# A transformer block on one core: first tiles normalized apart, the last outputs taken straight from PSUM, and the planner's costs adjusted

## The chip, the cores and the metric

The kernel runs on one core of one Trainium2 chip. The metric is the device time of one launch in microseconds (us). Lower is better. TensorE multiplies matrices into PSUM (PE in the profile; its weight loads are PEld), ScalarE (ACT) computes exponentials and tanh, VectorE (DVE) does elementwise work, GpSimd (POOL) one small power operation, SyncE (SP) issues transfers. The first measurement of the kernel before was 1119.43 us, the median of three runs (1118.68 to 1120.59).

## The reference

One block on x of 2048 tokens by 1024 channels, in bf16: layer norm, attention with 32 heads of 32 channels, output projection, residual; then layer norm, a feed-forward net of width 3584 with tanh-gelu, residual.

```python
x = A_x
h = x + _A_ref(_layernorm(x, axis=-1), A_wqkv, A_wo)
h2 = h + _B_ref(_layernorm(h, axis=-1), B_w1, B_b1, B_w2, B_b2)
return h2
# _A_ref: qkv = x @ wqkv; softmax(q k^T * 32**-0.5) v; @ wo
# _B_ref: gelu(x @ w1 + b1) @ w2 + b2
```

## The kernel before

The kernel is a graph of tasks, each with an engine, its instructions, and a **planned duration**. When the kernel is built, a list scheduler (the planner) walks through the graph with these durations and fixes the order of the instructions on each engine. The planner never measures: if an instruction takes longer or shorter than planned, the order stays and some engine waits.

```python
MM = 0.2195                       # a 512-column matmul; 0.0015 is added below

def c_act(n, ap_bias=False):      # ScalarE
    return 0.100 + (0.093 if ap_bias else 0.0) + n / 1200.0
...
def mm(g, lhsT, rhs, start, stop, reads, cols=(0, 512)):
    c0, c1 = cols
    occ = MM * (c1 - c0) / 512.0 + 0.0015
```

The planner gives TensorE a ready score matmul (`qk`) first, then a ready product with V (`pv`), then background work: projections, ffn1, ffn2. A score matmul becomes ready, in the plan, when the exponentials before it have freed their place in PSUM (the memory that TensorE writes to). So how much background work is let in between two score matmuls follows from how long the planner believes the exponentials take.

```python
if qk is not None:
    return qk
if pv is not None and not (...):
    ...
    return pv
if bg is not None:
    ...
    return bg
```

One attention round is one batch of 8 score matmuls, two exponentials of 128x1024 on ScalarE, a VectorE add of the halves of the result, 8 matmuls with V and 4 with ones (the softmax sums):

```python
pe(fns, 0.224, reads=[B_KT[g][r], B_QT[self.slot]], ..., kind="qk", mode="row")
for q in range(2):
    act(lambda a, u=u, q=q: a.activation(PT[:, s, 2*q:2*q+2, :], psum[:, 2*u:2*u+2, :], ACT.Exp, ...), 1024, ...)
```

The other places that the change touches, with cuts:

```python
for i in range(8):                # head: two tiles of x per step
    tts = [2 * i, 2 * i + 1]
    ln_tiles(tts, 0)
...
def ffn2(R, c, j, t, tail=False):
    grp = group(f"f2.{c}.{j}{t}")
    ...
    mm(grp, two_row[:, :], b2t[:, 512*j:512*j+512], True, False, ...)      # the bias as a matmul
    for fc in range(FC): mm(grp, gT[...], w[...], False, fc == FC - 1, ...)
    dve(... scalar_tensor_tensor(o, psum[:, grp.bank, :], 0.5, hch[...], ALU.mult, ALU.add) ...)
```

The softmax here doesn't subtract the row's maximum and nothing guards it: scores larger than these inputs give would overflow.

Of the kernel before, what the change touches and what calls it, by code (L numbers as in the profile page):

```python
# [7 lines left out]
ACT = mybir.ActivationFunctionType  # L8
# [304 lines left out]
def build_kernel(nc, A_x, A_wqkv, A_wo, B_w1, B_b1, B_w2, B_b2, out):  # L313
# [81 lines left out]
    pt_hi = top.cur  # L395
    NOT = 2
# [60 lines left out]
    MM = 0.2195  # L457
# [7 lines left out]
    def c_act(n, ap_bias=False):  # L465
        return 0.100 + (0.093 if ap_bias else 0.0) + n / 1200.0
# [38 lines left out]
    def dve(fn, occ, reads=(), writes=(), prio=0):  # L505
        return gr.add(E.DVE, fn, occ, 0.08, reads, writes, prio)
# [28 lines left out]
    cnt = {"ln": 0}  # L535

    def layer_norm(tiles, prio):
# [5 lines left out]
        for k, (x_ap, B_x, o_ap, B_o) in enumerate(tiles):  # L543
            for c in range(2):
                dve(lambda v, c=c, k=k, x_ap=x_ap: v.bn_stats(st_l[:, i + k, 6 * c:6 * c + 6], x_ap[:, 512 * c:512 * c + 512]),
                    0.68, reads=[B_x[c % len(B_x)]], writes=[B_stl[i + k]], prio=prio)
            dve(lambda v, k=k: v.bn_aggr(mv_l[:, i + k, :], st_l[:, i + k, :]), 0.2,
                reads=[B_stl[i + k]], writes=[B_mv[i + k]], prio=prio)
# [8 lines left out]
        for k, (x_ap, B_x, o_ap, B_o) in enumerate(tiles):  # L557
            dve(lambda e, k=k, x_ap=x_ap, o_ap=o_ap: e.tensor_scalar(
                o_ap, x_ap, mvr[:, i + k, :], rden[:, i + k, :], ALU.subtract, ALU.mult), 0.58,
                reads=B_x + [B_mvr[i + k], B_rden[i + k]], writes=[B_o], prio=prio)  # L560

    def transposes(g, src_ap, B_src, dst_ap, B_dst, evac):
        for dc in range(DC):
            grp_pe(g, lambda p, dc=dc: p.transpose(psb[:, g.bank, dc * P:(dc + 1) * P], src_ap[:, dc * P:(dc + 1) * P], ident[:]),  # L564
                   0.064, [B_src, B_ident], "full")
        if evac == "act":
            act(lambda a: a.activation(dst_ap, psb[:, g.bank, :].rearrange("p (dc t) -> p dc t", dc=DC), ACT.Copy), 1024,
                reads=[g.buf], writes=[B_dst], prio=-1)
        else:
            dve(lambda v: v.tensor_copy(dst_ap, psb[:, g.bank, :].rearrange("p (dc t) -> p dc t", dc=DC)), c_dve_ps(1024),  # L570
                reads=[g.buf], writes=[B_dst])
# [21 lines left out]
    def ln_tiles(tts, prio):  # L593
        layer_norm([x_slot(tt) + (xb[:, tt % NXB, :], B_xb[tt % NXB]) for tt in tts], prio)
# [55 lines left out]
    class Job:  # L650

        def __init__(self, g, c, bank=None, direct=False):
# [3 lines left out]
            self.needs = [t for b in B_V[g] for t in b.w] + B_OT[c % NOT][g].r + B_OT[c % NOT][g].w  # L656
            self.r = 0
            self.dens = []

        def round(self):  # L660
# [16 lines left out]
            pe(fns, 0.224, reads=[B_KT[g][r], B_QT[self.slot]], writes=[B_ps[2 * u + k] for u in us for k in range(2)],  # L677
# [5 lines left out]
            if not self.direct:  # L683
# [11 lines left out]
            t = pe(fns, 0.224, reads=B_PT[s] + [B_V[g][r]], writes=[self.buf], kind="pv", mode="col")  # L695
            pvs.append(t)
            job_of[t] = self
            self.dens.append((r, s if self.direct else z))
# [6 lines left out]
        def den(self, r, s):  # L705
            fns = []
            srcs = [PT[:, s, :, 0:256], PT[:, s, :, 256:512]] if self.direct else [PS[:, s, :, :]]
# [5 lines left out]
            pe(fns, 0.112 * len(srcs), reads=(B_PT[s] if self.direct else [B_PS[s]]) + [B_ones], writes=[self.buf], kind="pv", mode="col")  # L713

        def finish(self):
# [5 lines left out]
            dve(lambda v: v.tensor_copy(OS[:, f, :], psum[:, self.bank, 0:256]), c_dve_ps(256),  # L721
                reads=[self.buf], writes=[B_OS[f]], prio=-1)
# [4 lines left out]
            dve(lambda v: v.tensor_tensor(OT[:, c % NOT, g, :], OS[:, f, :], RT[:, f, :], ALU.mult), c_dve(256),  # L727
                reads=[B_OS[f], B_RT[f]], writes=[B_OT[c % NOT][g]])

# [90 lines left out]
    def ffn2(R, c, j, t, tail=False):  # L820
# [3 lines left out]
        grp = group(f"f2.{c}.{j}{t}")  # L824
        grp.soft = {d for _, _, d in ws}
        grp.dmas = [d for _, _, d in ws]
        grp.soft |= soft[c]
        grp.gate = [gate[c]]
        mm(grp, two_row[:, :], b2t[:, 512 * j:512 * j + 512], True, False, [B_two, B_b2t])
        for fc in range(FC):  # L830
            w, bw, _ = ws[fc // 4]
            mm(grp, gT[:, c % 2, fc, t * P:t * P + P], w[:, fc % 4, :], False, fc == FC - 1, [B_gT[c % 2][fc], bw])
        o, bo = R.os.next()
        dve(lambda v, j=j, t=t, o=o, grp=grp: v.scalar_tensor_tensor(
            o, psum[:, grp.bank, :], 0.5, hch[:, c % 2, t, 512 * j:512 * j + 512], ALU.mult, ALU.add),
            c_dve_ps(512), reads=[grp.buf, B_hch[c % 2][2 * t + j]], writes=[bo], prio=-2)
        dma(rows(out2, c, t, j), o, P * 1024, reads=[bo], prio=0)
# [31 lines left out]
    for i in range(8):  # L869
        tts = [2 * i, 2 * i + 1]  # L870
        ln_tiles(tts, 0)
# [92 lines left out]
    R2.os = Ring(ring(tail, "b_os", 2, 512, BF))  # L964
# [9 lines left out]
    for t in range(2):  # L974
        for j in range(2):
            wo_group(R2, L, j, t, ws[j])
        ln2_tile(R2, L, t, "act")
    for jt in F2:
        ffn2(R1, L - 1, *jt)
# [168 lines left out]
```

## Time and profile before

| | us |
|---|---|
| span of the profiled run (granted clock 1.000) | 1115.2 |
| first exponential starts | 16.9 |
| last exponential starts | 1044.0 |
| attention, first to last exponential | 1027.1 |
| tail, last exponential to the end | 71.2 |

I split the span at the first and the last exponential throughout, because these two marks exist in every version, whatever its order. The columns of a stage line are: the stretch, its length, then busy time and count for PE, PEld, DVE, ACT and POOL, the granted TensorE clock, the DMA share and GB/s. The kernel before, attention and tail:

```profile
16.90:1044.00 1027.10, 989.17 (x19567) 539.85 (x19568) 777.11 (x1388) 1009.90 (x1090) 13.52 (x20) 1.00 0.51 148
1044.00:1115.20 71.20, 67.77 (x469) 41.40 (x461) 35.02 (x53) 21.31 (x39) 1.09 (x2) 1.00 0.44 132
```

Subtract busy from length: in attention PE is idle 37.9 us and ACT 17.2, in the tail PE 3.4.

### The profile page before, as it was taken

The page shows a single profiled execution, that of the slowest core. Times are in us where ns is not written, and L with a number is a line of the kernel's source. Part 1 is how long each engine was busy: PE and PEld are TensorE (multiplying, and loading weights), DVE is VectorE, ACT ScalarE, POOL GpSimd, SP SyncE. Part 2 cuts the span into 40 slices and gives each one's busy share as a digit, 9 for nine tenths or more (in the row PEclk, how much of TensorE's full clock was granted, in tenths as well). Part 3 has the DMA queues.
Part 4 walks back from the last instruction along what each step waited for, and adds up shares of the span by engine and source line. Part 5 has one row for each costly group of instructions (what it writes and reads, how often), then busy time and mean ns, then how long its engine had stood idle before and what let it go on. Part 6 is the DMA issues. An engine that isn't in the chain of part 4 may idle for free.

```text
span 1115.2 us, 43935 instructions
## 1 busy us (share of the span) xinstructions
PE 1071.1 (96%) x20150; PEld 592.7 (53%) x20150; DVE 823.3 (74%) x1470; ACT 1035.3 (93%) x1131; POOL 18.0 (2%) x36
## 2 busy tenths in 40 slices
PE   8999999999999899999999999999999999999998
PEld 6646464644444555554565455455545554564483
DVE  7465756667767897788798788878887887797662
ACT  4889999999999999999999999999999999999550
POOL 1000000000000000000000000000000000000000
PEclk9999999999999999999999999999999999999999
DMA  6960100013234536375558464674747377688770
GB/s 190 200 162 4 40 4 3 4 48 106 66 101 139 166 110 209 100 242 146 176 157 247 131 200 145 189 230 121 241 117 226 113 230 209 202 229 239 229 241 20
DMA packets 248101, 165.38 MB, mean 148 GB/s; under 512 B 35947, under 2 KB 245867, under 8 KB 247916
## 3 DMA queue, kind: packets, MB, share of 16 engines
q1 hardware_dynamic: 247916, 162.57, 49.7%
q8 instruction: 158, 2.59, 1.0%
q14 instruction: 27, 0.22, 0.1%
HBM read 152.05 MB, written 7.34 MB: 143 GB/s over the span
## 4 chain that ended last, share of the span: by engine, by line
PE 73%; ACT 17%; DVE 7%; issue 1%; DMA 1%; POOL 0%; DVEq 0%; POOLq 0%
PE ps L495 28%; PE ps L498 21%; ACT PT L681 16%; PE ps L673 11%; PE ps L691 8%; PE ps L710 4%; DVE PS L686 3%; DVE gT L795 1%; PE ps L863 1%; ACT a_th L813 1%; DMA q_scratch<-stg 1%; PE ps L564 1%; DVE gT L814 0%; DVE a_sq L811 0%; DVE DT L719 0%
## 5 line engine op out<-in xcount | busy, mean ns | idle before, releaser
L681 ACT ACTIVATE PT<-ps 128x1024 bf16<-128x1024 f32 x1024 | 962.0, 1039 | 15.1 <-PE ps L673 8.8
L686 DVE TENSOR_TENSOR PS<-PT 128x1024 bf16<-128x1024 bf16 x496 | 328.4, 684 | 76.4 <-PE ps L710 40.1
L498 PE MATMUL ps<-hnT,w1r 128*128 128x256 bf16 x1632 | 208.0, 274 | 9.0 <-DVE gT L795 6.8
L673 PE MATMUL ps<-QT,KT 32*128 32x256 bf16 x4096 | 203.5, 273 | 10.9 <-ACT PT L681 9.6
L495 PE MATMUL ps<-w2r,gT 128*32 128x512 bf16 x2992 | 204.0, 381 | 0.2 <-DVE gT L814 0.2
L691 PE MATMUL ps<-PT,V 128*32 128x256 bf16 x4096 | 185.4, 274 | 4.6 <-ACT PT L681 2.7
L498 PEld LDWEIGHTS ps<-hnT,w1r 128*128 128x128 bf16 x1632 | 146.5, 98 | 63.2 <-issue 35.6
L673 PEld LDWEIGHTS ps<-QT,KT 32*128 32x128 bf16 x4096 | 61.0, 92 | 160.8 <-ACT PT L681 100.4
L710 PE MATMUL ps<-PS,ones 128*32 128x256 bf16 x1984 | 139.2, 276 | 0.9 <-DVE PS L686 0.5
L495 PE MATMUL ps<-xnT,Wall 128*32 128x512 bf16 x1888 | 128.9, 381 | 4.2 <-DVE KT L577 1.5
L691 PEld LDWEIGHTS ps<-PT,V 128*32 128x32 bf16 x4096 | 97.1, 96 | 55.0 <-issue 17.7
L495 PEld LDWEIGHTS ps<-w2r,gT 128*32 128x32 bf16 x2992 | 69.9, 96 | 64.2 <-issue 23.0
L795 DVE TENSOR_TENSOR gT<-ps,b1f 128x512 bf16<-128x512 f32 x98 | 67.2, 686 | 26.1 <-PE ps L498 25.3
L710 PEld LDWEIGHTS ps<-PS,ones 128*32 128x32 bf16 x1984 | 51.7, 95 | 42.6 <-DVE PS L686 23.8
L495 PEld LDWEIGHTS ps<-xnT,Wall 128*32 128x32 bf16 x1888 | 45.0, 96 | 47.5 <-issue 14.0
L814 DVE SCALAR_TENSOR_TENSOR gT<-a_th,gT 128x1024 bf16<-128x1024 f32 x49 | 59.7, 1219 | 13.5 <-ACT a_th L813 13.5
L495 PE MATMUL ps<-w1r,OT 128*32 128x512 bf16 x896 | 59.7, 381 | 2.7 <-DVE hch L755 1.1
L811 DVE SCALAR_TENSOR_TENSOR a_sq<-a_sq,gT 128x1024 bf16<-128x1024 bf16 x49 | 59.8, 1220 | 0.7
L495 PE MATMUL ps<-Wall,xnT 128*32 128x256 bf16 x1536 | 51.4, 273 | 1.3 <-DVE KT L577 0.8
L813 ACT ACTIVATE a_th<-a_sq 128x1024 f32<-128x1024 bf16 x49 | 51.9, 1060 | 0.4 <-DVE a_sq L811 0.2
L719 DVE STREAM_TRANSPOSE DT<-ps 128x256 f32<-128x256 f32 x64 | 28.6, 447 | 24.2 <-PE ps L710 24.2
L495 PEld LDWEIGHTS ps<-Wall,xnT 128*32 128x32 bf16 x1536 | 38.3, 97 | 9.2 <-issue 7.2
(81 smaller groups left out, 625.0 us busy)
## 6 DMA issues: line engine op xcount, KB each, us to landing
w2r<-in_B_w_dram SPq DMA_DIRECT2D x105, 512.0 KB, 6.1
w1r<-in_B_w_dram SPq DMA_DIRECT2D x102, 512.0 KB, 4.5
w1r<-in_A_wo_dram SPq DMA_DIRECT2D x28, 512.0 KB, 4.6
wk<-in_B_w_dram SPq DMA_DIRECT2D x9, 512.0 KB, 5.5
xrb<-in_A_x_dram SPq DMA_DIRECT2D x16, 256.0 KB, 4.2
Wall<-in_A_wqkv_dram SPq DMA_DIRECT2D x16, 256.0 KB, 5.2
wv<-in_B_w_dram SPq DMA_DIRECT2D x8, 512.0 KB, 7.3
a_x<-in_A_x_dram SPq DMA_DIRECT2D x28, 128.0 KB, 3.7
```

The lines of the kernel that those rows point to most:

```text
L495: fns.append(lambda p, j=j: p.matmul(dst(32 * j, 32 * j + 32), lhsT[:, 32 * j:32 * j + 32], rhs, start=start, stop=stop, tile_position=(0, ...
L498: t.alt = [lambda p: p.matmul(dst(0, P), lhsT, rhs, start=start, stop=stop, skip_group_check=True)]
L673: fns.append(lambda p, i=i, hh=hh, r0=r0: p.matmul(psum[:, 2 * us[hh // 2] + hh % 2, 256 * i:256 * i + 256], KT[r0:r0 + 32, g, 256 * r + P ...
L681: act(lambda a, u=u, q=q: a.activation(PT[:, s, 2 * q:2 * q + 2, :], psum[:, 2 * u:2 * u + 2, :], ACT.Exp, bias=0.0, scale=SCALE), 1024, r ...
L686: dve(lambda v: v.tensor_tensor(PS[:, z, :, :], PT[:, s, :, 0:256], PT[:, s, :, 256:512], ALU.add), c_dve(1024, 2), reads=B_PT[s], writes= ...
L691: fns.append(lambda p, i=i, hh=hh: p.matmul(psum[32 * hh:32 * hh + 32, self.bank, 0:256], V[:, g, 2 * r + i, 32 * hh:32 * hh + 32], PT[:, ...
L710: fns.append(lambda p, i=i, hh=hh, src=src: p.matmul(psum[32 * hh:32 * hh + 32, self.bank, 256:512], ones32[:, :], src[:, hh, :], start=False,
L719: dve(lambda v: v.transpose(DT[:, f, :], psum[:, self.bank, 256:512]), c_dve_ps(256), reads=[self.buf], writes=[B_DT[f]], prio=-1)
L795: gate[c] = dve(lambda v, xh=xh, fc=fc, grp=grp: v.tensor_tensor(xh, psum[:, grp.bank, :].rearrange("p (f n) -> p f n", f=2), b1f[:, fc:fc ...
L811: dve(lambda v: v.scalar_tensor_tensor(v4(sq), v4(sq), C2, xh, ALU.add, ALU.mult), c_dve(n), reads=[b_sq] + b_xh, writes=[b_sq], prio=1)
L813: act(lambda a: a.activation(th, sq, ACT.Tanh, bias=0.0, scale=K2 / 2), n, reads=[b_sq], writes=[b_th], prio=-1, kind="tanh")
L814: t = dve(lambda v: v.scalar_tensor_tensor(xh, v4(th), 1.0, xh, ALU.add, ALU.mult), c_dve(n), reads=[b_th] + b_xh, writes=b_xh, prio=1)
```

## The change

Its stated intent: bring the first projection forward (normalize the first tile alone, let idle ScalarE compute the sums of the second), shorten the path behind the last exponential, take the bias matmuls out of the TensorE-bound tail, and end on a smaller eviction. The diff also moves the planner's durations closer to measured ones, which its headline does not say. Cut to its core:

```diff
-    MM = 0.2195
+    MM = 0.2140
-        return 0.100 + (0.093 if ap_bias else 0.0) + n / 1200.0      # c_act
+        return 0.090 + (0.093 if ap_bias else 0.0) + n / 1200.0
-            pe(fns, 0.224, ...kind="qk") ; pe(fns, 0.224, ...kind="pv") ; pe(fns, 0.112 * len(srcs), ...)
+            pe(fns, 0.217, ...)          ; pe(fns, 0.217, ...)          ; pe(fns, 0.1085 * len(srcs), ...)
...
+            if k in on_act:                                  # sums of one tile on ScalarE
+                for f, fn in enumerate((ACT.Copy, ACT.Square)):
+                    act(... a.activation(junk, x_ap, fn, scale=1.0, accum_out=st_l[:, i + k, f:f + 1]) ...)
+                (three small VectorE steps: mean, -mean^2, variance)
-        ln_tiles(tts, 0)
+        if i == 0:
+            ln_tiles(tts[:1], LEAD_PRIO)
+            first = ln_tiles(tts[1:], LEAD_PRIO, (0,))
+        else:
+            ln_tiles(tts, 0, (), first)
...
+            direct = self.direct or (self.final and r == 7)  # last head: no add of halves on VectorE
+            (last head: output multiplied from PSUM, no copy OS)
...
+        n = 256 if tail and (j, t) == F2[-1] else 512        # last group in two halves
+            if not tail:
                 mm(grp, two_row[:, :], b2t[:, 512 * j:512 * j + 512], True, False, ...)
+            h_ap, b_h = (hb[:, t, at], B_hb[t]) if tail else (hch[...], ...)   # hb = hch + b2, made on VectorE
```

More of the change, by code (lines that the diff above doesn't have):

```diff
@@ L395, in build_kernel @@
     pt_hi = top.cur
+    junk = PT[:, NPT - 1, 0:2, :]
+    B_junk = B_PT[NPT - 1][0]
     NOT = 2
@@ L503, in act, with dve @@
         return gr.add(E.Activation, fn, c_act(n, ap_bias), 0.14, reads, writes, prio, kind)
-    def dve(fn, occ, reads=(), writes=(), prio=0):
-        return gr.add(E.DVE, fn, occ, 0.08, reads, writes, prio)
+    def dve(fn, occ, reads=(), writes=(), prio=0, after=()):
+        return gr.add(E.DVE, fn, occ, 0.08, reads, writes, prio, after=after)
     def pool(fn, occ, reads=(), writes=(), prio=0):
@@ L535, in build_kernel, with layer_norm @@
     cnt = {"ln": 0}
-    def layer_norm(tiles, prio):
+    LEAD_PRIO = -4
+    def layer_norm(tiles, prio, on_act=(), after=()):
         n = len(tiles)
@@ L543, in layer_norm @@
         for k, (x_ap, B_x, o_ap, B_o) in enumerate(tiles):
+            if k in on_act:
+                for f, fn in enumerate((ACT.Copy, ACT.Square)):
+                    act(lambda a, k=k, x_ap=x_ap, f=f, fn=fn: a.activation(
+                        junk, x_ap, fn, scale=1.0, accum_out=st_l[:, i + k, f:f + 1]), 1024 + 112,
+                        reads=B_x, writes=[B_stl[i + k], B_junk], prio=-1)
+                dve(lambda v, k=k: v.tensor_scalar(mv_l[:, i + k, 0:1], st_l[:, i + k, 0:1], 1.0 / D, None, ALU.mult), 0.12,
+                    reads=[B_stl[i + k]], writes=[B_mv[i + k]], prio=prio)
+                dve(lambda v, k=k: v.scalar_tensor_tensor(st_l[:, i + k, 2:3], mv_l[:, i + k, 0:1], -1.0, mv_l[:, i + k, 0:1], ALU.mult, ALU.mult),
+                    0.12, reads=[B_mv[i + k]], writes=[B_stl[i + k]], prio=prio)
+                dve(lambda v, k=k: v.scalar_tensor_tensor(mv_l[:, i + k, 1:2], st_l[:, i + k, 1:2], 1.0 / D, st_l[:, i + k, 2:3], ALU.mult, ALU.add),
+                    0.12, reads=[B_stl[i + k]], writes=[B_mv[i + k]], prio=prio)
+                continue
             for c in range(2):
                 dve(lambda v, c=c, k=k, x_ap=x_ap: v.bn_stats(st_l[:, i + k, 6 * c:6 * c + 6], x_ap[:, 512 * c:512 * c + 512]),
-                    0.68, reads=[B_x[c % len(B_x)]], writes=[B_stl[i + k]], prio=prio)
+                    0.68, reads=[B_x[c % len(B_x)]], writes=[B_stl[i + k]], prio=prio, after=after)
             dve(lambda v, k=k: v.bn_aggr(mv_l[:, i + k, :], st_l[:, i + k, :]), 0.2,
@@ L557, in layer_norm @@
         for k, (x_ap, B_x, o_ap, B_o) in enumerate(tiles):
-            dve(lambda e, k=k, x_ap=x_ap, o_ap=o_ap: e.tensor_scalar(
+            t = dve(lambda e, k=k, x_ap=x_ap, o_ap=o_ap: e.tensor_scalar(
                 o_ap, x_ap, mvr[:, i + k, :], rden[:, i + k, :], ALU.subtract, ALU.mult), 0.58,
                 reads=B_x + [B_mvr[i + k], B_rden[i + k]], writes=[B_o], prio=prio)
+        return [t]
     def transposes(g, src_ap, B_src, dst_ap, B_dst, evac):
@@ L569, in transposes @@
         else:
-            dve(lambda v: v.tensor_copy(dst_ap, psb[:, g.bank, :].rearrange("p (dc t) -> p dc t", dc=DC)), c_dve_ps(1024),
+            dve(lambda v: v.tensor_copy(dst_ap, psb[:, g.bank, :].rearrange("p (dc t) -> p dc t", dc=DC)), c_dve_ps(512),
                 reads=[g.buf], writes=[B_dst])
@@ L591, in x_tile, with ln_tiles @@
         return dma(ap, x2[tt * P:(tt + 1) * P, :], P * D * 2, writes=b, prio=prio)
-    def ln_tiles(tts, prio):
-        layer_norm([x_slot(tt) + (xb[:, tt % NXB, :], B_xb[tt % NXB]) for tt in tts], prio)
+    def ln_tiles(tts, prio, on_act=(), after=()):
+        return layer_norm([x_slot(tt) + (xb[:, tt % NXB, :], B_xb[tt % NXB]) for tt in tts], prio, on_act, after)
     def tr_tile(tt, evac):
@@ L656, in __init__ @@
             self.needs = [t for b in B_V[g] for t in b.w] + B_OT[c % NOT][g].r + B_OT[c % NOT][g].w
+            self.final = (g, c) == (G - 1, NC - 1)
             self.r = 0
@@ L676, in round @@
                         start=True, stop=True, tile_position=(r0, 0)))
-            pe(fns, 0.224, reads=[B_KT[g][r], B_QT[self.slot]], writes=[B_ps[2 * u + k] for u in us for k in range(2)],
+            pe(fns, 0.217, reads=[B_KT[g][r], B_QT[self.slot]], writes=[B_ps[2 * u + k] for u in us for k in range(2)],
                kind="qk", mode="row")
@@ L682, in round @@
                     1024, reads=[B_ps[2 * u], B_ps[2 * u + 1]], writes=[B_PT[s][q]], kind="exp")
-            if not self.direct:
+            direct = self.direct or (self.final and r == 7)
+            if not direct:
                 z = unit["ps"] % NPS
@@ L694, in round @@
                         tile_position=(0, 32 * hh), skip_group_check=True))
-            t = pe(fns, 0.224, reads=B_PT[s] + [B_V[g][r]], writes=[self.buf], kind="pv", mode="col")
+            t = pe(fns, 0.217, reads=B_PT[s] + [B_V[g][r]], writes=[self.buf], kind="pv", mode="col")
             pvs.append(t)
             job_of[t] = self
-            self.dens.append((r, s if self.direct else z))
+            self.dens.append((r, s if direct else z, direct))
             if len(self.dens) == 2:
@@ L703, in round, with den @@
                 self.finish()
-        def den(self, r, s):
+        def den(self, r, s, direct):
             fns = []
-            srcs = [PT[:, s, :, 0:256], PT[:, s, :, 256:512]] if self.direct else [PS[:, s, :, :]]
+            srcs = [PT[:, s, :, 0:256], PT[:, s, :, 256:512]] if direct else [PS[:, s, :, :]]
             for i, src in enumerate(srcs):
@@ L712, in den @@
                         stop=r == 7 and i == len(srcs) - 1, tile_position=(0, 32 * hh), skip_group_check=True))
-            pe(fns, 0.112 * len(srcs), reads=(B_PT[s] if self.direct else [B_PS[s]]) + [B_ones], writes=[self.buf], kind="pv", mode="col")
+            pe(fns, 0.1085 * len(srcs), reads=(B_PT[s] if direct else [B_PS[s]]) + [B_ones], writes=[self.buf], kind="pv", mode="col")
         def finish(self):
@@ L720, in finish @@
                 reads=[self.buf], writes=[B_DT[f]], prio=-1)
-            dve(lambda v: v.tensor_copy(OS[:, f, :], psum[:, self.bank, 0:256]), c_dve_ps(256),
-                reads=[self.buf], writes=[B_OS[f]], prio=-1)
+            if not self.final:
+                dve(lambda v: v.tensor_copy(OS[:, f, :], psum[:, self.bank, 0:256]), c_dve_ps(256),
+                    reads=[self.buf], writes=[B_OS[f]], prio=-1)
             dve(lambda v: v.reciprocal(RB[:, f, :], DT[:, f, :].rearrange("p (b j) -> p b j", j=32)[:, :, 0]), 0.15,
@@ L726, in finish @@
                 reads=[B_RB[f]], writes=[B_RT[f]])
-            dve(lambda v: v.tensor_tensor(OT[:, c % NOT, g, :], OS[:, f, :], RT[:, f, :], ALU.mult), c_dve(256),
-                reads=[B_OS[f], B_RT[f]], writes=[B_OT[c % NOT][g]])
+            dve(lambda v: v.tensor_tensor(OT[:, c % NOT, g, :], psum[:, self.bank, 0:256] if self.final else OS[:, f, :], RT[:, f, :], ALU.mult),
+                c_dve_ps(256), reads=[self.buf if self.final else B_OS[f], B_RT[f]], writes=[B_OT[c % NOT][g]])
     def wblock(R, src_ap):
@@ L823, in ffn2 @@
         ws = w2s[c, j]
-        grp = group(f"f2.{c}.{j}{t}")
-        grp.soft = {d for _, _, d in ws}
-        grp.dmas = [d for _, _, d in ws]
-        grp.soft |= soft[c]
-        grp.gate = [gate[c]]
-        mm(grp, two_row[:, :], b2t[:, 512 * j:512 * j + 512], True, False, [B_two, B_b2t])
-        for fc in range(FC):
-            w, bw, _ = ws[fc // 4]
-            mm(grp, gT[:, c % 2, fc, t * P:t * P + P], w[:, fc % 4, :], False, fc == FC - 1, [B_gT[c % 2][fc], bw])
-        o, bo = R.os.next()
-        dve(lambda v, j=j, t=t, o=o, grp=grp: v.scalar_tensor_tensor(
-            o, psum[:, grp.bank, :], 0.5, hch[:, c % 2, t, 512 * j:512 * j + 512], ALU.mult, ALU.add),
-            c_dve_ps(512), reads=[grp.buf, B_hch[c % 2][2 * t + j]], writes=[bo], prio=-2)
-        dma(rows(out2, c, t, j), o, P * 1024, reads=[bo], prio=0)
+        n = 256 if tail and (j, t) == F2[-1] else 512
+        for h in range(512 // n):
+            grp = group(f"f2.{c}.{j}{t}.{h}")
+            grp.soft = {d for _, _, d in ws}
+            grp.dmas = [d for _, _, d in ws]
+            grp.soft |= soft[c]
+            grp.gate = [gate[c]]
+            if not tail:
+                mm(grp, two_row[:, :], b2t[:, 512 * j:512 * j + 512], True, False, [B_two, B_b2t])
+            at = slice(512 * j + n * h, 512 * j + n * h + n)
+            for fc in range(FC):
+                w, bw, _ = ws[fc // 4]
+                mm(grp, gT[:, c % 2, fc, t * P:t * P + P], w[:, fc % 4, n * h:n * h + n], tail and fc == 0, fc == FC - 1,
+                   [B_gT[c % 2][fc], bw], cols=(0, n))
+            o, bo = R.os.next()
+            h_ap, b_h = (hb[:, t, at], B_hb[t]) if tail else (hch[:, c % 2, t, at], B_hch[c % 2][2 * t + j])
+            dve(lambda v, o=o, h_ap=h_ap, grp=grp: v.scalar_tensor_tensor(
+                o[:, 0:n], psum[:, grp.bank, 0:n], 0.5, h_ap, ALU.mult, ALU.add),
+                c_dve_ps(n), reads=[grp.buf, b_h], writes=[bo], prio=-2)
+            dma(out2[256 * c + P * t:256 * c + P * t + P, at], o[:, 0:n], P * n * 2, reads=[bo], prio=0)
     def mixed(R, c1, c2, plan):
@@ L963, in build_kernel @@
     R2.th = Ring(ring(tail, "b_th", 3, 1024, F32))
-    R2.os = Ring(ring(tail, "b_os", 2, 512, BF))
+    R2.os = Ring(ring(tail, "b_os", 3, 512, BF))
+    hb, B_hb = sb(tail, "hb", [P, 2, D], F32, 2)
+    b2b, B_b2b = sb(tail, "b2b", [P, D], BF)
     slots = []
@@ L977, in build_kernel @@
         ln2_tile(R2, L, t, "act")
+    dma(b2b[:], B_b2.rearrange("(o d) -> o d", o=1).broadcast_to((P, D)), P * D * 2, writes=[B_b2b], prio=1)
+    for t in range(2):
+        dve(lambda v, t=t: v.tensor_tensor(hb[:, t, :], hch[:, L % 2, t, :], b2b[:], ALU.add), c_dve(1024),
+            reads=B_hch[L % 2][2 * t:2 * t + 2] + [B_b2b], writes=[B_hb[t]], prio=2)
     for jt in F2:
```

## The prediction

> **What bounds the kernel now.** I read the page first, then busy time by stage, then the two ends in order of time, then the waits of the middle.
>
> Part 1 of the page (busy time of each engine over the 1115.2 us span), and one row of part 2 (40 slices of the span, in tenths):
>
> ```profile
> PE 1071.1 (96%) x20150; PEld 592.7 (53%) x20150; DVE 823.3 (74%) x1470; ACT 1035.3 (93%) x1131; POOL 18.0 (2%) x36
> ...
> ACT  4889999999999999999999999999999999999550
> ```
>
> TensorE (PE) is busy 96% of the span and ScalarE (ACT) 93%, so two engines are nearly full at once. The ACT row says where: it is poor in the first slice and in the last two and a half. Busy time by stage (start:end, length, then PE, PEld, DVE, ACT, POOL) puts numbers on that:
>
> ```profile
> 60.00:1047.00 987.00, 952.19 (x19019) 515.36 (x19015) 755.86 (x1319) 974.55 (x1043) 9.39 (x14) 1.00 0.49 146
> 1047.00:1115.20 68.20, 65.27 (x428) 40.47 (x427) 34.33 (x52) 20.32 (x37) 1.09 (x2) 1.00 0.45 136
> ```
>
> Three stages, three limits. In the middle (987 us) ACT is idle 12.5 us and PE 34.8 us: there is nearly nothing to win by a local repair, and no part of the change removes work there. The tail (68 us) is PE alone: ACT is a third busy, PE 65.3 of 68.2. The head is a latency chain. In order of time it reads (start, length, engine, line, operation):
>
> ```profile
> 3.49 2.01 DVE L545 BATCH_NORM_STATS2 st<-xrb 128x6 f32<-128x512 bf16 x3 [3.49 <-DMA xrb<-in_A_x_dram]
> ...
> 6.97 0.71 POOL L553 TENSOR_TENSOR denb<-tb,cexp 128x2 bf16<-128x2 bf16 x1 [4.24 <-DVE tb L551]
> 8.10 0.69 DVE L545 BATCH_NORM_STATS2 st<-xrb 128x6 f32<-128x512 bf16 x1 [1.15 <-DMA xrb<-in_A_x_dram]
> 8.71 0.15 DVE L556 RECIPROCAL rden<-denb 128x2 f32<-128x2 bf16 x1
> ...
> 9.44 0.99 DVE L558 TENSOR_SCALAR xb<-xrb,mvr,rden 128x1024 bf16<-128x1024 bf16 x2
> ...
> 10.95 1.94 ACT L567 ACTIVATE xnT<-ps 128x1024 bf16<-128x1024 bf16 x2 [8.94 <-PE ps L564]
> ...
> 16.89 1.94 ACT L681 ACTIVATE PT<-ps 128x1024 bf16<-128x1024 f32 x2
> ```
>
> Both first tiles go through one normalization: four statistics in a row on VectorE, one square root on GpSimd for both (done at 7.68), then a reciprocal that comes only at 8.71, because VectorE, in order, sits behind a statistic of tile 2 that waits for its transfer until 8.10. The transposed tiles are out of PSUM at 12.89, the first exponential starts at 16.89.
>
> The end of the tail:
>
> ```profile
> 1105.84 0.38 PE L498 MATMUL ps<-b2t,two_row 128*128 128x512 bf16 x1
> ...
> 1111.24 1.03 PE L498 MATMUL ps<-wk,gT 128*128 128x512 bf16 x4
> 1112.30 0.69 DVE L834 SCALAR_TENSOR_TENSOR b_os<-ps,hch 128x512 bf16<-128x512 f32 x1 [5.50 <-PE ps L498]
> ```
>
> The bias of ffn2 is a matmul of its own, one per group, and after the last matmul comes one 512-column eviction (0.69) and a store of 128 KB, which lands 1.7 us after it is issued at 1113.02.
>
> [...]20 such matmuls span 4.48 us with 0.38 for one, so (4.48 - 0.38) / 19 = 0.216. [...]The trace has 1.039 for one exponential; 15 in a row took 13.92 in the chain, 0.928 apart. [...]the 256-column copy out of PSUM in the trace takes 0.38. [...]
>
> **The change part by part.**
>
> *Head.* Tile 0 alone: two statistics end at about 4.83 (3.49 + 2 x 0.67), aggregate 0.2, two small VectorE steps 0.35, one-tile square root 0.54 (the tail has that form), reciprocal 0.15, normalize 0.53: 6.6. Tile 1 lands by 4.8 (its statistics did not wait). ACT, idle until 10.95, does Copy and Square with sums: 2 x about 1 us, done at 6.8. Then three small VectorE steps 0.45, two more 0.35, root 0.54, reciprocal and normalize 0.7: 8.85. Eight transposes 0.6 and an eviction of 1.0: 10.5, against 12.89. That is 2.4 us at best; [...]the in-order VectorE queue will take some, so I put 1.8 on the start of the first projections. Later tiles now wait for tile 1, which takes 1.3 us of statistics out of VectorE's early gaps; but tiles 2 and 3 were normalized only at 16.63, held by a query eviction queued ahead of them, and should now come earlier. From about 28 us PE is full with work that is there, so a shift survives. I count **-1.5**.
>
> *End of attention.* The last round of the last head sums both halves on PE instead of a VectorE add (0.69, from 1045.02) and the last output is multiplied straight from PSUM, without a 0.38 copy. Added: four 256-column matmuls side by side, 0.11. The latency falls by about 1 us, but PE fills most of that time with other work; it stands still for 0.50 + 0.17 + 0.35 us between 1045.5 and 1049.2. I count **-0.6**.
>
> *Bias on VectorE.* Four 512-column matmuls go, 4 x 0.216 = 0.86 us of PE in the tail. The first ffn2 group already waits 0.36 us at 1092.45 for the last gelu, so its 0.22 becomes wait: **-0.65**. The two adds put in [...]fall where VectorE idles between 1058.2 and 1062.8, and their results are needed only at 1093.
>
> *Last group in two banks.* 56 matmuls of 256 columns for 28 of 512. The tail's 256-column run takes (7.15 - 0.27) / 63 = 0.109 each, so 6.12 against 28 x 0.216 = 6.05: +0.07. [...]The store is halved: -0.1. Sum **-0.3**.
>
> These four give **-3.05 us**.
>
> *Not in the headline: the planner's constants.* The kernel orders its instructions by a cost model run at build time, and the diff changes that: matmul 0.2195 to 0.2140 plus 0.0015, attention rounds 0.224 to 0.217, ACT overhead 0.100 to 0.090, one transposed eviction halved. So the order of all 20150 matmuls can move. The matmul is now 0.2155 against 0.216 measured (before 0.221: 2.4% too slow). ACT goes from 0.953 to 0.943 against 0.928, still 1.6% too slow. The VectorE add of a round, 0.618 in the model, is (2.63 - 0.69) / 3 = 0.65 in the trace: it was relatively 7% too cheap beside PE and is now 5% too cheap. The ratio of ACT to PE was nearly right before and becomes 2% worse. The waits such errors cause are in view: PE waited in the middle 6.8 us for gelu inputs, 6.7 and 2.7 for exponentials:
>
> ```profile
> PE ps L498 <- DVE gT L795: 6.8, 14, 0.9
> PE ps L673 <- ACT PT L681: 6.7, 17, 0.8
> PE ps L691 <- ACT PT L681: 2.7, 7, 0.5
> ```
>
> A plan nearer to the truth may win back a part; a new order may as well lose some. An author keeps what ran faster, so I put **-2.5**, with 5 us either way: a choice, not a sum.
>
> **The rivals.** (1) *The head's gain is swallowed*: VectorE normalizes later tiles no earlier, PE waits there, and head gives 0. For: VectorE works almost without gap from 8 to 41 us. Against: PE has a backlog from 28 us, and the last projections run at 52.8 us, long after the last tile's transposes are issued. It would make some 1115.5. (2) *The order of the middle decides*: the four local gains are 3 us, a reordering that moves the middle by half a percent drowns them, and the result is anywhere from 1106 to 1121. For: 34.8 us of PE idle there. Against: ACT has only 12.5 us, so no large win. (3) *Square needs another table*: a load of 1.28 us as the one at 0.72, and a second to return, would eat the head's gain. For: only one load is in the trace. [...]It would make about 1116. (4) *The tail becomes bound by gelu*: the first group's wait grows from 0.36 to 0.6; already counted.
>
> **Range and chances.** 1119.43 - 3.05 - 2.5 = 1113.9. The 8-in-10 range is 1106.0 to 1119.0: the lower end is the four gains in full and 9 to 10 us from a better order, the upper the local gains nearly undone by the order. Faster by 2% would be under 1097.5: 22 us, more than ACT's idle time in the middle and the local gains together. Chances 0.02, 0.97, 0.01.
>
> **What would show it.** First exponential at about 15.2 instead of 16.89, two ACT passes near 4.8, one table load. No bias matmuls after the last ffn1, four fewer 512-column matmuls there, 56 of 256 columns in the last group, a last eviction near 0.42, the tail from the last exponential about 1.5 us shorter. In the middle, PE and ACT idle by stage and the waits for L795's and L681's counterparts: if they are unchanged, the order was neutral and the time is 1116.4. The prediction is wrong if the middle moves by more than 6 us either way, or if the head's shift is gone by 60 us.

Passages of the prediction that rested on figures or mechanisms that no trace or run of this case shows are cut, and the cuts are marked. Its sum: -1.5, -0.6, -0.65 and -0.3 make the -3.05 us of the local parts, and with -2.5 for the planner's constants 1119.43 becomes 1113.9. The -0.3 of the last group is +0.07, -0.27 for the last eviction and -0.1 for the store. The trace gives the same -0.27: the 512-column eviction at 1112.30 takes 0.69 us, a 256-column cast out of PSUM at 15.63 takes 0.42. The -0.1 was the author's estimate, which nothing before the change showed. The two adds of the bias took 1.22 us each in the changed kernel. The "20 such matmuls" have 512 columns and start at 1095.27.

## More of the kernel before

At about 416 to 424 us TensorE runs short of work:

```profile
416.00:420.00 4.00, 2.59 (x53) 0.89 (x45) 3.48 (x7) 4.00 (x5) 0.00 (x0) 1.00 0.03 6
420.00:424.00 4.00, 3.36 (x37) 2.40 (x33) 3.41 (x7) 4.00 (x6) 0.00 (x0) 1.00 0.17 48
```

Of four microseconds PE works 2.59. In this execution the clock stayed at 1.00.

## The result, and the profile after

The changed kernel took **1122.05 us** (median of 4 runs, 1119.74 to 1123.35), the kernel before in the same rounds 1120.01. The ratio is 1.0017, with a 95% interval of 0.9996 to 1.0039. Ratios here are the mean time of one kernel's fast runs over that of the other's of the same rounds, so they are not quite the ratio of the medians. A second measurement on another chip gave 1.0043 (1.0028 to 1.0059). "The same within 2%" held, and the time did not: it lies 3 us above the range.

The head of the changed kernel, in order of time:

```profile
4.21 1.06 ACT L549 ACTIVATE PT<-xrb 128x1024 bf16<-128x1024 bf16 x1 [2.21 <-DMA xrb<-in_A_x_dram]
5.18 0.19 ACT L549 ACTIVATION_READ_ACCUMULATOR PT<-xrb 128x1 f32 x1
...
8.31 2.02 PE L888 MATMUL ps<-b2t,ident 128*128 128x256 bf16 x17
8.50 0.55 DVE L573 TENSOR_SCALAR xb<-xrb,mvr,rden 128x1024 bf16<-128x1024 bf16 x1
...
10.17 0.61 PE L580 MATMUL ps<-ident,xb 128*128 128x128 bf16 x8
10.81 1.02 ACT L583 ACTIVATE xnT<-ps 128x1024 bf16<-128x1024 bf16 x1 [1.28 <-PE ps L580]
...
15.91 1.93 ACT L698 ACTIVATE PT<-ps 128x1024 bf16<-128x1024 f32 x2
```

The two ScalarE passes are there, with a short extra instruction that reads the accumulator. Tile 1 is normalized by 9.05, but its transposes start only at 10.17: 17 of the matmuls that the code issues only to keep TensorE busy (its kind "warm", L888) stand ahead of them in TensorE's queue until 10.33. The first exponential comes at 15.9, against 16.9. These are two single executions, and this mark scatters: over all profiles it lies at 15.7 to 17.1 with the new head (13 profiles, mean 16.5; the changed kernel's second profile has 16.8) and at 16.9 to 17.7 with the old one (5 profiles, mean 17.3). So the head's change is worth about 0.8 us at this mark.

The end of the tail:

```profile
1114.83 0.60 PE L500 MATMUL ps<-wk,gT 128*128 128x256 bf16 x4
1115.47 0.42 DVE L859 SCALAR_TENSOR_TENSOR b_os<-ps,hb 128x256 bf16<-128x256 f32 x1 [2.63 <-PE ps L500]
```

The last eviction takes 0.42, and no bias matmul stands in the tail. So the local parts look as designed. The stages tell where the time went. Attention and tail of the changed kernel:

```profile
15.90:1051.40 1035.50, 996.04 (x19642) 542.02 (x19644) 779.69 (x1392) 1014.50 (x1090) 14.34 (x21) 1.00 0.51 147
1051.40:1118.00 66.60, 62.82 (x476) 42.25 (x472) 36.35 (x54) 21.54 (x39) 1.10 (x2) 1.00 0.46 142
```

Head 1.0 us shorter, **attention 8.4 us longer** (1035.5 against 1027.1), tail 4.6 us shorter: 2.8 us in all. PE was busy 6.9 us longer in attention and 4.95 us shorter in the tail. Of the latter some 0.8 is the bias (the 0.86 of the prediction less 0.07 for the halves), so about 4 us of background work moved from the tail into attention. The rest of the longer busy time in attention, some 2.8 us, fits a lower clock. The mean granted clock was 0.997 here and 1.000 in the profile before, and it fell in the stretch that was thin already:

```profile
416.00:420.00 4.00, 1.62 (x40) 0.87 (x40) 2.71 (x4) 4.00 (x5) 0.00 (x0) 0.87 0.06 16
420.00:424.00 4.00, 3.48 (x45) 1.09 (x38) 1.84 (x5) 3.07 (x5) 0.00 (x0) 0.70 0.00 0
```

PE works 1.62 of four microseconds, against 2.59, and its clock is cut (at 418.96). In finer slices of 2 us the clock reads 0.50 in both places where this happened (402 to 404 and 420 to 422 us). Both low stretches last 3.41 us; a batch of 8 score matmuls takes 0.61 us in them, against 0.40 at full clock. TensorE was not idle before them, only thin: 2.38 and 1.31 us busy in the 3.41 us before the fall, the longest gap in them 0.50 and 1.10. How thin is too thin does not come out: the kernel before was busy only 1.71 of the 3.41 us from 24.55, and its clock stayed at 1.00. Two such stretches lose at most 2 x 3.41 x 0.5 = 3.4 us of TensorE work (an estimate from the trace's lengths). Slices of low clock stand in other traces too (`e2_consts` 0.50 at 420 to 424, `after_again` 0.59 there, `c_act` 0.59 at 740 to 744).

### The profile page after: what moved, and what is told of

It reads as the page before. It is cut to its first block, busy times and chain, and to the rows that moved or that the text cites. A ratio compares the mean times of both kernels' runs of the same rounds, so it can differ in the third digit from the quotient of the medians.

```text
span 1118.0 us, 44121 instructions
## 1 busy us (share of the span) xinstructions
PE 1072.1 (96%) x20225; PEld 594.9 (53%) x20229; DVE 825.6 (74%) x1475; ACT 1042.5 (93%) x1135; POOL 19.2 (2%) x37
## 4 chain that ended last, share of the span: by engine, by line
PE 81%; ACT 11%; DVE 6%; issue 1%; POOL 0%; DVEq 0%; POOLq 0%
PE ps L497 31%; PE ps L500 23%; PE ps L690 12%; ACT PT L698 11%; PE ps L709 9%; PE ps L728 5%; DVE PS L704 2%; PE ps L888 1%; DVE gT L814 1%; PE ps L580 1%; DVE stg L593 0%; DVE a_os L859 0%; DVE gT L833 0%; ACT a_th L832 0%; DVE a_sq L830 0%
## 5 line engine op out<-in xcount | busy, mean ns | idle before, releaser
L698 ACT ACTIVATE PT<-ps 128x1024 bf16<-128x1024 f32 x1024 | 966.6, 1034 | 18.6 <-PE ps L690 10.5
L704 DVE TENSOR_TENSOR PS<-PT 128x1024 bf16<-128x1024 bf16 x495 | 328.1, 683 | 78.5 <-PE ps L728 42.5
L690 PE MATMUL ps<-QT,KT 32*128 32x256 bf16 x4096 | 204.0, 273 | 9.3 <-ACT PT L698 8.2
L497 PE MATMUL ps<-w2r,gT 128*32 128x512 bf16 x3056 | 210.3, 382 | 1.4 <-DVE gT L833 1.2
L690 PEld LDWEIGHTS ps<-QT,KT 32*128 32x128 bf16 x4096 | 60.8, 92 | 162.3 <-ACT PT L698 99.4
L709 PEld LDWEIGHTS ps<-PT,V 128*32 128x32 bf16 x4096 | 96.4, 96 | 58.4 <-issue 17.3
```

What stands on the lines that cost most here:

```text
L497: fns.append(lambda p, j=j: p.matmul(dst(32 * j, 32 * j + 32), lhsT[:, 32 * j:32 * j + 32], rhs, start=start, stop=stop, tile_position=(0, ...
L690: fns.append(lambda p, i=i, hh=hh, r0=r0: p.matmul(psum[:, 2 * us[hh // 2] + hh % 2, 256 * i:256 * i + 256], KT[r0:r0 + 32, g, 256 * r + P ...
L698: act(lambda a, u=u, q=q: a.activation(PT[:, s, 2 * q:2 * q + 2, :], psum[:, 2 * u:2 * u + 2, :], ACT.Exp, bias=0.0, scale=SCALE), 1024, r ...
L704: dve(lambda v: v.tensor_tensor(PS[:, z, :, :], PT[:, s, :, 0:256], PT[:, s, :, 256:512], ALU.add), c_dve(1024, 2), reads=B_PT[s], writes= ...
L709: fns.append(lambda p, i=i, hh=hh: p.matmul(psum[32 * hh:32 * hh + 32, self.bank, 0:256], V[:, g, 2 * r + i, 32 * hh:32 * hh + 32], PT[:, ...
```

## The experiments

A fact settled beforehand, without the chip: with the planner's old constants, the local changes leave the middle's order as it was. A comparison of TensorE's order, some 2300 rows, finds 83 differing rows (those of both sides counted) for the local changes alone, all in the head and the tail. When this document was checked, the planners of the recorded kernels were run once more and counted with slightly different rows: of 2469, 63 differ for the local changes alone and 1962 for the new constants alone. So the two can be taken apart cleanly. Theory A: the local gains are real and the reordered middle gives them back. Theory B: later waits swallow the local gains.

**First job: the parts.** `e1_local` is the changed kernel with the six old constants:

```diff
-    MM = 0.2140
+    MM = 0.2195
-        return 0.090 + (0.093 ...
+        return 0.100 + (0.093 ...
 (and 0.224, 0.112, and the two VectorE costs as before)
```

> The changed kernel with the planner's old constants. Its instruction order differs from the kernel before only in the first rows and in the tail (83 of 2294 rows of TensorE), so the middle is the old one. Theory A (the local gains are real, the reordered middle gives them back): 2.5 to 3.5 us faster than before, ratio 0.997 to 0.998, granted clock as the kernel before has it, last exponential about 1 us earlier than before. Theory B (the local gains are swallowed by later waits): within 0.7 us of before, ratio above 0.9993.

Measured: 0.998 (0.9965 to 0.9995), 1117.12 us against 1119.0. `e2_consts` is the converse, the kernel before with the new constants only.

> The kernel before with only the planner's new constants: head and tail as before, the middle reordered. Theory A: 4 to 6 us slower than before, ratio 1.0035 to 1.0055, the last exponential some 7 us later, and windows of half clock in the middle as the changed kernel has (mean clock under 1.000). Theory B: within 1.5 us of before, the changed kernel being slow for another reason.

Measured: 1.0031 (1.0016 to 1.0046), last exponential at 1053.6 against 1044.0, mean clock of its runs 0.994 to 0.997, where the kernel before had 0.997 or 0.998. Theory A holds, a little below its own numbers for `e2_consts` (1.0035 at least); B falls. The same job took the local part apart. `e3_tail` is `e1_local` without the head's and the last head's change:

```diff
-        if i == 0: ... ln_tiles(tts[1:], LEAD_PRIO, (0,)) ...
+        ln_tiles(tts, 0)
-            self.final = (g, c) == (G - 1, NC - 1)
+            self.final = False
```

> Only the change of the tail (bias of the last ffn2 on VectorE, last group in two halves) on the kernel before; all orders up to the tail are the same. By the prediction's sum 0.65 + 0.3 = about 1 us faster, ratio 0.9991. If the tail's weight is hidden by the gelu chain: 0.3 us or less.

Measured: 0.9988 (0.9972 to 1.0003). The interval holds zero, but the trace shows the tail at 70.5 us against 71.2. `e4_lead` keeps only the head's change (bias matmul, one bank and `final = False` restored).

> Only the change of the head on the kernel before, with the old constants; the middle keeps its order. The traces showed the first exponential 1.0 us earlier (15.9 against 16.9). If that shift survives to the end: 1 us faster, ratio 0.9991. If a later wait swallows it: 0, the last exponential at the same time as before.

Measured: 0.9995 (0.9978 to 1.0012); first exponential at 15.7, last at 1044.3, in a run with clock 0.998. So the head's gain is visible at the front and not resolved at the end. `e5_final` keeps only the last head's change; it ran in the last job.

> Only the change of the last head's output on the kernel before, old constants; only 14 rows of TensorE differ, at the end of attention. The prediction put 0.6 us on it: ratio 0.9995. If TensorE has other work there and the latency is hidden: 0, ratio 1.000.

Measured: 0.9999 (0.9986 to 1.0012): nothing that these rounds can resolve. The three parts sum to 0.9982, close to the 0.998 measured together.

**Second job: the clock, and which constant.** `after_again` is the changed kernel, for comparison on the same chip. `fill_after` is the same order with the score matmuls of two jobs issued twice, in the stretch where PE starves:

```diff
+            if (g, self.c) in ((0, 3), (1, 3)):
+                one = list(fns)
+                fns[-1] = lambda p, one=one: [f(p) for f in one[-1:] + one][-1]
```

> The changed kernel once more, beside the next run and on the same chip. Both theories: ratio to before 1.001 to 1.003; of its executions most with 2 to 4 windows of half clock (mean clock 0.995 to 0.997), against about one for the kernel before (0.998).

> The changed kernel in its own order, but each score matmul of the two heads' jobs in which TensorE starves (about 396 to 424 us) is issued twice: 128 matmuls more, the same results, the planner not told. Theory C (half of the loss is the throttled clock, entered because TensorE is too idle at 400 to 424): the windows of half clock in this stretch vanish, mean clock 0.998 to 1.000, and in spite of 16 x 0.22 = 3.5 us more TensorE work the kernel is 1 to 3 us faster than the changed one. Theory D (the low clock follows from something else, or the stretch is bound by ScalarE anyway): clock as in the changed kernel, and the time the same or up to 3 us longer.

Measured: `after_again` 1.0043, more than the 1.003 expected, `fill_after` 1.0049 (1.0036 to 1.0063). In the profile of `fill_after` no slice of 400 to 430 us is below full clock (the two low spots are at 24 to 32 and 828 to 836), and the mean clock of its runs rose from 0.9942 to 0.9958. That fits Theory C's cause of the low clock, but does not settle it: the clock stayed under the 0.998 that C expected, the rise is about twice its standard error (six runs each), and one profile without a low stretch can be chance, since `e1_local` and `e4_lead`, which share one order there, show none and one. The expected 1 to 3 us did not come: whatever the filler saved, it cost again. On the gain Theory C is wrong.

`c_pe` is `e1_local` with only TensorE's constants new, `c_act` with only ScalarE's:

```diff
 c_pe:   MM = 0.2140, rounds 0.217, sums 0.1085       (c_act stays 0.100)
 c_act:  return 0.090 + (0.093 ...                     (TensorE's stay old)
```

> The local changes with the old constants, and of the constants only those of TensorE as new (matmul 0.2140, rounds 0.217, sums 0.1085). If the TensorE constants do the harm: as the changed kernel, 3 to 5 us slower than the local changes alone, ratio to before 1.001 to 1.003. If they do not: ratio 0.997 to 0.999.

> The local changes with the old constants, and of the constants only that of ScalarE as new (0.090). If it does the harm: ratio to before 1.001 to 1.003; if not: 0.997 to 0.999. If both this and the TensorE constants alone cost 2 us or more, the harm is not in one constant but in leaving the old order.

Measured: `c_pe` **1.0136** (1.0117 to 1.0155), 1133.89 us, mean clock 0.990; `c_act` 0.9993 (0.9978 to 1.0009). The TensorE constants do the harm, far more than the 1.001 to 1.003 expected and more than the whole change, and ScalarE's new constant undoes a part. Yet the matmul's new constant is closer to the measured duration (0.2155 against 0.216). That gave the next theory. Theory R: what counts is the planned cost of ScalarE relative to TensorE. With exponential 0.100 + 1024/1200 = 0.953 and matmul 0.2195 + 0.0015 = 0.221 the old ratio is 4.31; I took 0.925 and 0.216 as measured, that is 4.28; the changed kernel plans 4.38, `c_pe` 4.42. (The 0.925 is too long. In the kernel before, 961 pairs of exponentials follow each other without other ScalarE work between; the median is 0.920 us from start to start, and most pairs are at 0.90 or 0.92. So the measured ratio is 4.18 to 4.26.) Theory S: the old constants had been tuned, and any other order loses.

**Third job: ratio or reorder.** One constant each:

```diff
 f_act072 (from the changed kernel):  return 0.090 + ...  ->  return 0.072 + ...
 o_act128 (from e1_local):            return 0.100 + ...  ->  return 0.128 + ...
 t_mm_lo, t_mm_hi (from e1_local):    MM = 0.2195         ->  MM = 0.2190, MM = 0.2200
```

> The changed kernel with one constant moved: ScalarE overhead 0.072 instead of 0.090, so that one exponential costs 0.925 in the plan, as measured, against a matmul of 0.2155, as measured. Theory R (what counts is the ratio of the planned cost of ScalarE to that of TensorE: 4.31 with the old constants, 4.38 in the changed kernel, 4.42 with new TensorE constants alone, 4.28 measured): the ratio is 4.29 here, so the loss goes: 0.996 to 0.999 of the kernel before. Theory S (any order other than the old, tuned one costs 3 to 6 us): 1.002 to 1.006.

> The local changes with the old TensorE constants, and ScalarE overhead raised from 0.100 to 0.128: ratio 4.44, as far off as with the new TensorE constants alone (4.42), but reached from the other side. Theory R: about as slow as that run, 1.010 to 1.018 of the kernel before. If instead the absolute TensorE constants did the harm (their padding stood for losses that the plan does not know): within 1.004.

> The local changes with the old constants, the matmul 0.2190 instead of 0.2195 (0.2%). It reorders 934 rows of TensorE, but moves the ratio by 0.01 only. Theory R: as the local changes alone, 0.997 to 0.999 of the kernel before. Theory S: 1.001 to 1.006, as with any reorder.

> The same with 0.2200. Theory R: 0.997 to 0.999. Theory S: 1.001 to 1.006. If the two differ from each other by over 3 us, a part of the effect is the luck of a single order, and its size is seen here.

Measured: `f_act072` **0.9924** (0.9911 to 0.9936), `o_act128` 1.0175 (1.0161 to 1.0189), `t_mm_lo` 0.9964, `t_mm_hi` 0.994. Theory S falls at once: three reorders out of four are faster. Theory R's signs hold on both sides: `o_act128` moves ScalarE's constant alone and loses as `c_pe` did, so neither TensorE's constants as such nor their relation to VectorE's are needed for the loss. R's numbers were too timid: `f_act072`, `t_mm_hi` and, barely, `t_mm_lo` came out faster than it said. By the ratios the two tiny shifts differ from each other by 2.7 us, and `t_mm_hi` from `e1_local` by 4.5: that is about the luck of a single order. The chip adds to it: the jobs ran on different chips, and the changed kernel itself had 1.0017 on one and 1.0043 on another, 2.9 us apart.

The profile shows where the time goes. The group of the exponentials (count, busy us and mean ns, then the idle time of ScalarE just before them and what ended most of it), first of the kernel before:

```profile
L681 ACT ACTIVATE PT<-ps 128x1024 bf16<-128x1024 f32 x1024 | 962.0, 1039 | 15.1 <-PE ps L673 8.8 <-PE ps L691 1.8
```

of the changed kernel:

```profile
L698 ACT ACTIVATE PT<-ps 128x1024 bf16<-128x1024 f32 x1024 | 966.6, 1034 | 18.6 <-PE ps L690 10.5 <-PE ps L709 1.9
```

of `o_act128`:

```profile
L698 ACT ACTIVATE PT<-ps 128x1024 bf16<-128x1024 f32 x1024 | 973.3, 1033 | 29.9 <-PE ps L690 20.1 <-PE ps L709 1.2
```

and of `f_act072`:

```profile
L698 ACT ACTIVATE PT<-ps 128x1024 bf16<-128x1024 f32 x1024 | 956.1, 1056 | 14.9 <-PE ps L690 8.4 <-PE ps L709 4.1
```

L673 and L690 are the score matmuls. If the planner thinks an exponential longer than it is, relative to a matmul, it puts more background matmuls between two score batches than fit beside two exponentials. The score matmul then comes late and ScalarE stands still: 20.1 us on this wait, against 8.8. The changed kernel has 10.5 here and 13.5 in its second profile, `c_pe` 13.7.

Idle time alone misleads, though: `f_act072` has hardly less of it than the kernel before (14.9 us against 15.1), and its attention is 7.1 us shorter. Exponentials overlap when they follow each other at once (mean length 1.04 us, but 0.90 or 0.92 from start to start), so one that comes a little late first loses its overlap, and only then does idle time appear: of those 961 pairs in the kernel before, 103 start over 0.935 us apart and still overlap, in the changed kernel 113. Busy and idle time of the group belong together: 977.1 us before, 985.2 in the changed kernel (+8.1, of the 8.4 by which its attention is longer), 1003.2 in `o_act128`, 971.0 in `f_act072`.

**Fourth job: the other side, and the local parts in a good order.** `f_act081` and `f_act055` are the changed kernel with 0.081 and 0.055, `b_act072` is the kernel before with the new constants and 0.072.

> The changed kernel with ScalarE overhead 0.081, half way between 0.090 and 0.072; planned ratio 4.34. Theory R (time follows the ratio): between the two, 0.995 to 1.000 of the kernel before, attention (first to last exponential) of 1022 to 1033 us. Scatter alone: outside that.

> The same with 0.055, below the measured cost; ratio 4.22. Theory R with a best point: attention no longer than with 0.072 (1020 us), but a longer tail, as TensorE carries more work past it; in all 0.994 to 1.000 of the kernel before. If shorter planned exponentials only help: below 0.991.

> The kernel before with the new constants but ScalarE overhead 0.072, no local change. If the local changes are worth the same 2 to 3 us in this order: 0.994 to 0.996 of the kernel before, against 0.9924 with them.

Measured: `f_act081` 0.9975 (0.9961 to 0.9988), `f_act055` 1.0018 (1.0004 to 1.0032), `b_act072` 0.9934 (0.9913 to 0.9955). The last two lie outside what was expected, `f_act055` slower and `b_act072` slightly faster. The orders by planned ratio (the last column was counted by running the kernels' planners without the chip: background tasks, of one or four matmuls each, placed before the last score batch):

| run | ratio planned | time against before | attention us | tail us | background tasks placed |
|---|---|---|---|---|---|
| f_act055 | 4.22 | 1.0018 | 1014.3 | 88.5 | 3663 |
| c_act | 4.27 | 0.9993 | 1021.4 | 78.5 | 3726 |
| f_act072 | 4.29 | **0.9924** | 1020.0 | 72.2 | 3755 |
| b_act072 | 4.29 | 0.9934 | 1019.6 | 73.5 | 3755 |
| t_mm_hi | 4.30 | 0.9940 | 1025.1 | 71.0 | 3759 |
| e1_local | 4.31 | 0.9980 | 1026.3 | 70.0 | 3767 |
| kernel before | 4.31 | 1 | 1027.1 | 71.2 | 3767 |
| t_mm_lo | 4.32 | 0.9964 | 1030.9 | 66.9 | 3778 |
| f_act081 | 4.34 | 0.9975 | 1031.4 | 66.8 | 3779 |
| changed kernel | 4.38 | 1.0017, 1.0043 | 1035.5 | 66.6 | 3784 |
| e2_consts | 4.38 | 1.0031 | 1036.4 | 68.2 | 3784 |
| c_pe | 4.42 | 1.0136 | 1046.4 | 69.9 | 3813 |
| o_act128 | 4.44 | 1.0175 | 1051.8 | 70.5 | 3813 |

The last column is the step that was argued above: the higher the planned ratio, the more background work stands among the score matmuls. Attention grows almost steadily with it, the tail shrinks to a floor at about 66.6 us (in the last two rows it is longer again, at a mean clock of 0.93 and 0.92 in the tail), and the sum has a best point in between. That this point is the measured ratio is not shown: the best three orders plan 4.29 and 4.30, and the two that plan the measured 4.18 to 4.26 most closely, `f_act055` and `c_act`, are 10 and 8 us slower than `f_act072`. The scatter of single orders is some 3 to 5 us (`e1_local` against `t_mm_hi`). At low ratios, the background work that did not get into attention waits until ScalarE is idle; the stages of `f_act055` show it:

```profile
16.20:1030.50 1014.30, 977.42 (x19248) 527.19 (x19247) 774.80 (x1384) 993.97 (x1089) 14.21 (x21) 1.00 0.50 144
1030.50:1119.00 88.50, 85.54 (x574) 53.99 (x578) 43.45 (x63) 22.44 (x40) 1.10 (x2) 1.00 0.58 180
```

PE in the tail is busy 85.5 us, against 67.8 in the kernel before. That the sum of PE's busy time is 6 us above that of the kernel before is not explained by its clock alone (0.997 over 1119 us loses 3.4 us, an estimate); this stays open.

`f_act072` beats both kernels: 1111.95 us (1110.37 to 1112.93) against 1120.53 of the kernel before in the same rounds, 0.8% faster, with the right result. Beside it, `b_act072` without any local change has 0.9934, so in this order the local parts are worth about 0.1%, and the intervals of the two overlap.

**How much of the loss is the clock.** Over all 125 executions of these jobs, with one offset per kernel and one for the kernel before on each chip, 0.001 less mean granted clock goes with 1.0 us more (0.001 of 1120 us is 1.1 us of TensorE's time). The changed kernel's runs average 0.9944, those of `e1_local` 0.9975, the kernel before 0.998. By that fit some 3 of the 5.6 us between the changed kernel and `e1_local` (1.0030, the mean of its two ratios, less 0.998) go with the clock. The idle time of ScalarE before the exponentials is 18.6 us in the one and 14.0 in the other, so the rest has a place too, but the two overlap: the slow clock also makes the score matmuls end later (0.61 us for a batch, against 0.40). The split is a fit, not an intervention: the one intervention, `fill_after`, brought the clock up a little and gained nothing.

## Why the prediction was wrong

It predicted 1113.9 us, 1106 to 1119; measured were 1122.05. The step that failed is the term "Not in the headline: the planner's constants", with its words "An author keeps what ran faster, so I put **-2.5**, with 5 us either way: a choice, not a sum." It measured +0.31% alone (`e2_consts`), about **+3.5 us**, and about +5.6 us on top of the local changes. Its sign was wrong, and its bounds were too narrow: over the constants tried here the order is worth -7 us (`b_act072`) to +20 us (`o_act128`, with the local gains in it).

- **The working pointed the right way, and was set aside.** The same paragraph says "The ratio of ACT to PE was nearly right before and becomes 2% worse." That sentence names the cause; what was missing was the step from "2% worse" to a sign: more background work among the score matmuls, later exponentials. Instead the guess about the author took its place. (Its 0.928 us from exponential to exponential is 13.92 / 15 and counts the last one in full; the starts are 0.916 apart there.)
- **Idle time was taken for all that an order can win.** "ACT has only 12.5 us, so no large win": `f_act072` won some 8 us with hardly less idle time, because late exponentials also lose overlap, which counts as busy.
- **Local parts: predicted -3.05 us, measured -2.2 (0.998)**, with an interval of -3.9 to -0.6. The sum is resolved; of its terms none is, by time alone.
- **Head: predicted -1.5.** The first exponential came 1.0 us earlier in the profiles compared (0.8 in the mean of all), not 1.7; the end gained 0.6 with an interval that holds zero. The sum missed these "warm" matmuls: 17 of them stood ahead of tile 1's transposes. It also gave ScalarE's sums no accumulator read (0.19 and 0.18 us), which the earlier start at 4.21 made up for.
- **End of attention: predicted -0.6, measured 0.0** (0.9999). TensorE had other work, as the second half of that step feared. The step also misread the profile: of its "0.50 + 0.17 + 0.35 us" only the 0.50 is a wait of PE; the other two are waits of the weight loads (PEld), beside which the matmuls ran on.
- **Bias and last group: predicted -0.95.** In the traces the tail of `e3_tail` is 0.7 us shorter than that of the kernel before; by time 0.9988, -1.3 us with an interval of -3.1 to +0.3. The 0.36 us at 1092.45, by which the step cut the gain from 0.86 to 0.65, is again a wait of PEld; PE shows no gap there. The last eviction was 0.42, as put. The store of half the size (64 KB after 128) landed in 1.6 us after 1.7: -0.1, as put.
- **Rivals.** Rival 2, "the order of the middle decides", was the right one, and its span, 1106 to 1121, was nearly right. Rival 3 fell: Copy, Square, Exp and Tanh ran with one table load in the trace (1.28 us at 0.72). Rival 4 was not seen: the weight loads waited 0.31 us for the last gelu, after 0.36, and PE not at all.
- **Not in the prediction at all:** the granted clock. The profile before showed 1.000, and of its other 11 executions in the first job nine read 0.998 and two 0.997. The profiled execution was a good one.

## What to carry to other kernels

Where a build-time planner orders the instructions of two engines that are both nearly full, as here, the ratio of its costs can matter more than each cost: change them together, try values on both sides, since the truest costs need not give the fastest order, and measure the order apart from the local edits. Read a change of constants as a change of the whole program; look in the order that they give, or at least in the ratio, before a guess about why someone made it. And look at the granted clock of all executions, not of the profiled one, in stretches where TensorE is thin (here it fell to 0.50 after 1.31 us of work in 3.41).
